# Loading the first query columns early, and scheduling with more slack behind VectorE and GpSimd, in an attention-and-mixer kernel

## The chip, the cores and the metric

The kernel runs on one core of one Trainium2 chip. The time is the device time of one execution in microseconds; the span of a profile (first to last instruction) is about 1.8 us shorter. The engines are called by the profile's names: PE (TensorE's matmuls), PEld (its weight loads), DVE (VectorE), ACT (ScalarE), POOL (GpSimd) and SP (the queue that issues most DMAs). "L829" is line 829 of the kernel.

## The reference

Sequence 2048, width 512, 32 heads of 16, everything in bf16. Two branches share x and are mixed by a gate:

```python
def reference(A_x, A_wqkv, A_wo, B_x, B_w1, B_w2, B_w3, B_w4, gate_w):
    x = A_x
    g = _sigmoid((x * gate_w).sum(-1, keepdims=True))
    a = _A_ref(x, A_wqkv, A_wo)             # 32-head attention, softmax over 2048 keys
    b = _B_ref(x, B_w1, B_w2, B_w3, B_w4)   # layernorm, w1, gelu, shift, w2, layernorm, w3, gelu, w4
    return g * a + (1 - g) * b
```

The attention's 32 x 2048 x 2048 exponentials set the size of the problem. Everything else is fitted between them.

## The kernel before

The kernel contains its own model of the engines. While it is being built, this model plays all work out in time, with a hold (how long an engine is busy) and a latency (from then until users may start) for each job, and a set of settings for each of 65 stages of the score tiles. Instructions are emitted in the order of the model's start times. Each engine's list then stands in that order; the model's times are gone, only the order stays.

```python
    def try_engine(self, e):
        # ... picks the job with the best (prio, ready, seq) among those whose inputs and buffers are there
        self.emit(self.t, j.fn)
        self.t_free[e] = self.t + j.hold
        # ...
        self.push(self.t + j.hold + j.lat, lambda: self.finish_job(j))     # users may start from here

    def dve(hold, deps, fn, **kw):
        return sim.add(Job("DVE", hold, 150.0, deps, fn, **kw))

    def act(hold, deps, fn, **kw):
        return sim.add(Job("ACT", hold, 160.0, deps, fn, **kw))

    def gp(hold, deps, fn, **kw):
        return sim.add(Job("POOL", hold, 110.0, deps, fn, port=True, **kw))
```

The scores (L829) go to two kinds of PSUM buffers. Those in "psA" get their exponential on ACT (L909). Those in "ring" are evicted by DVE (L935) as the bits of an exponential, which DVE (L971) or POOL (L974) then finishes by shifts. Both results, PA and PD, feed the value products (L1005). The first loads, and the matmuls that only keep PE busy while they run:

```python
    xa, xb = (start(e, 3000.0, lambda q, a=a: q.dma_start(out=x_sb[:, a:a + 2, :], in_=x_src(0, a, a + 2)))
              for e, a in (("SP", 0), ("ACT", 2)))
    dl_w["k0"] = start("ACT", 2300.0, col(W("k"), D, D + 128))
    dl_w["q0"] = start("ACT", 2300.0, col(wq, 0, 128))
    j_x1 = [start("SP", 4900.0, lambda q: q.dma_start(out=x_sb[:, 4:8, :], in_=x_src(1, 0, 4)))]
    # ...
    def warm_pe():
        for _ in range(8):
            nc.tensor.matmul(sim_ring[RING - 1][:, 0:384], lhsT=zero[:, 0:P], rhs=zero[:], start=True, stop=True)
```

The softmax here doesn't subtract the row's maximum and nothing guards it: scores larger than these inputs give would overflow.

Of the kernel before, what the change touches and what calls it, by code (L numbers as in the profile page):

```python
# [10 lines left out]
ACT = mybir.ActivationFunctionType  # L11
# [223 lines left out]
def kernel(  # L235
# [18 lines left out]
    S, D = x_flat.shape  # L254
# [7 lines left out]
    COL = True  # L262
# [23 lines left out]
        P1_PRIO=0.414,  # L286
        S_PRIO=0.38,
        GP2=0.0,
        GP3=1.0,
        DVE_STOP=6,  # L290
        DVE_STOP_L=8,
        URG=5,
        URG_L=17,
        DVE_ALONE=2,
        EARLY=68,
        SL=(45, 60),
        IDLE_NS=537,
        PD_LOW=0,
        PA_LOW=0,
        DVE_WAIT=3,  # L300
        AHEAD=9,
        AHEAD2=9,
        PV_FULL=0.916,
        PV_IDLE=0.37,
        PRESS=27,
        MAXU=9,
        ROT=0, DUE_SH=0, AT_SH=0,
    )
    SEG = 32
    STAGES = {0: {'DUE_SH': -20, 'AHEAD': 7, 'GP2': 0.35}, 2: {'S_PRIO': 0.324}, 3: {'SL': (125, 60), 'AT_SH': 120}, 4: {'ROT': 2, 'DVE_STOP': 7, 'DUE_SH': -8, 'GP2': 0.35}, 5: {'ROT': 2}, 6: {'AHEAD': 8, 'GP2': 0.1, 'P1_PRIO': 0.54}, 7: {'DVE_STOP': 9, 'P1_PRIO': 0.53}, 8: {'DUE_SH': 40, 'URG_L': 19, 'AT_SH': 60}, 9: {'GP2': 0.35, 'DVE_WAIT': 2, 'EARLY': 20, 'PV_IDLE': 0.245}, 10: {'GP3': 0.6}, 11: {'IDLE_NS': 706, 'GP2': 0.35}, 13: {'PV_IDLE': 0.414, 'SL': (5, 60), 'IDLE_NS': 296}, 14: {'GP3': 0.9, 'AT_SH': 120}, 15: {'ROT': 3, 'P1_PRIO': 0.554, 'PV_FULL': 0.948}, 16: {'GP2': 0.1, 'EARLY': 141}, 17: {'AT_SH': 10}, 18: {'GP2': 0.35, 'MAXU': 4}, 19: {'GP2': 0.35, 'P1_PRIO': 0.522, 'SL': (165, 180), 'DVE_WAIT': 2}, 20: {'EARLY': 145, 'S_PRIO': 0.286, 'GP2': 0.1}, 21: {'EARLY': 145, 'S_PRIO': 0.286, 'GP2': 0.1}, 22: {'AHEAD': 11, 'AT_SH': 10, 'EARLY': 51}, 23: {'AT_SH': 10}, 24: {'ROT': 2, 'URG': 3, 'GP3': 0.8}, 25: {'PD_LOW': 2}, 26: {'SL': (125, 60), 'DUE_SH': 40, 'S_PRIO': 0.248, 'AHEAD2': 8}, 27: {'ROT': 1, 'URG_L': 15, 'AHEAD': 12}, 28: {'PRESS': 21, 'P1_PRIO': 0.544, 'S_PRIO': 0.282}, 29: {'PV_IDLE': 0.462, 'DVE_STOP': 4}, 30: {'GP3': 0.9, 'PRESS': 21}, 31: {'GP3': 0.6}, 32: {'DVE_WAIT': 6, 'ROT': 2, 'DUE_SH': 40}, 34: {'DUE_SH': 40, 'DVE_ALONE': 2, 'GP3': 0.6}, 35: {'IDLE_NS': 471, 'DUE_SH': 20, 'DVE_STOP': 5, 'MAXU': 3}, 36: {'GP2': 0.1, 'PRESS': 14}, 37: {'DVE_ALONE': 2, 'DVE_STOP': 3, 'EARLY': 31, 'PA_LOW': 3}, 38: {'PD_LOW': 3, 'EARLY': 55, 'PA_LOW': 2, 'URG': 7}, 39: {'S_PRIO': 0.456, 'AHEAD2': 7, 'EARLY': 155, 'ROT': 1}, 40: {'PA_LOW': 3, 'DVE_ALONE': 2, 'GP3': 0.8}, 41: {'URG': 8, 'URG_L': 19}, 42: {'URG_L': 19, 'PRESS': 39, 'ROT': 1}, 43: {'GP3': 0.8}, 44: {'PD_LOW': 1}, 45: {'DVE_WAIT': 2, 'AHEAD2': 10}, 46: {'GP3': 0.6}, 47: {'DUE_SH': -40, 'EARLY': 79, 'MAXU': 9, 'PA_LOW': 2}, 48: {'DVE_ALONE': 300, 'ROT': 1}, 49: {'AT_SH': 120, 'P1_PRIO': 0.475}, 50: {'IDLE_NS': 896, 'PD_LOW': 2, 'ROT': 2, 'PA_LOW': 1}, 51: {'PD_LOW': 1, 'URG': 6, 'DVE_ALONE': 150, 'IDLE_NS': 830}, 52: {'PRESS': 53, 'EARLY': 6, 'IDLE_NS': 668, 'PV_FULL': 0.848}, 53: {'AHEAD': 12, 'AT_SH': 10, 'PA_LOW': 2, 'ROT': 3}, 54: {'DVE_STOP_L': 6, 'GP3': 0.9}, 55: {'DUE_SH': -40, 'PV_IDLE': 0.253, 'DVE_STOP_L': 10, 'PA_LOW': 2}, 56: {'SL': (25, 60), 'PA_LOW': 2}, 57: {'ROT': 1, 'SL': (85, 60)}, 58: {'GP3': 0.8, 'PD_LOW': 3, 'URG_L': 19}, 59: {'GP2': 0.1}, 60: {'DUE_SH': -20, 'GP3': 0.6, 'P1_PRIO': 0.409}, 61: {'GP2': 0.2}, 62: {'DVE_STOP_L': 10, 'MAXU': 6, 'PA_LOW': 2, 'AHEAD2': 11}, 63: {'DVE_STOP_L': 6, 'MAXU': 6, 'ROT': 1}, 64: {'DVE_STOP_L': 6, 'MAXU': 6, 'SL': (165, 180)}}  # L310
    K = SimpleNamespace(**BASE)


# [11 lines left out]
    def slots(name, n, shape, dt=BF16, where=const):  # L325
        return [where.tile(shape, dt, name=f"{name}{i}") for i in range(n)]
# [3 lines left out]
    wq = const.tile([P, KT, D], BF16, name="wq")  # L330
# [34 lines left out]
    sim = Sim({  # L365
        **{f"psA{w}{n}": slots(f"psA{n}", 1, [P, 512 * w], F32, ps) for n, w in enumerate(WIDTHS)},
        "ring": sim_ring,
        "PA": slots("PA", NPA, [P, 512 * max(WIDTHS)]),
        "token": list(range((NPD - 1) // 3)),
        "PD": slots("PD", NPD, [P, 1024], U16),  # L370
        "w": slots("w", NW, [P, KT, D]),
        "xnT": slots("xnT", 2, [P, KT, 512]),
        "xn": slots("xn", 2, [P, D]),
# [12 lines left out]
    })  # L386

    def dve(hold, deps, fn, **kw):
        return sim.add(Job("DVE", hold, 150.0, deps, fn, **kw))

    def act(hold, deps, fn, **kw):
        return sim.add(Job("ACT", hold, 160.0, deps, fn, **kw))

    def gp(hold, deps, fn, **kw):
        return sim.add(Job("POOL", hold, 110.0, deps, fn, port=True, **kw))

    def dma(lat, deps, fn, hold=450.0, **kw):
        return sim.add(Job("SP", hold, lat - hold, deps, fn, **kw))
# [12 lines left out]
    def W(name):  # L411
        return wb[name].slot

    j_xT, j_x, dl_w = {}, [], {}
# [9 lines left out]
    def start(eng, lat, fn, hold=530.0):  # L424

        job = sim.add(Job("SP", 1, 0.0, [], None, prio=-1))
        sim.jobs["SP"].remove(job)
        t = issue.get(eng, 700.0)
        issue[eng] = t + hold
        sim.push(t + hold + lat, lambda: sim.finish_job(job))  # L430
        sim.pending -= 1
        fn(nc.sync if eng == "SP" else nc.scalar)
        return job

    col = lambda w, n0, n1: (lambda q: q.dma_start(out=w[:, :, n0 % D:n1 if n1 <= D else (n1 - 1) % D + 1],
                                                   in_=wrows(A_wqkv[:, n0:n1])))
    xa, xb = (start(e, 3000.0, lambda q, a=a: q.dma_start(out=x_sb[:, a:a + 2, :], in_=x_src(0, a, a + 2)))
              for e, a in (("SP", 0), ("ACT", 2)))
    j_x0 = [xa, xb]
    dl_w["k0"] = start("ACT", 2300.0, col(W("k"), D, D + 128))  # L440
    dl_w["q0"] = start("ACT", 2300.0, col(wq, 0, 128))
    j_x1 = [start("SP", 4900.0, lambda q: q.dma_start(out=x_sb[:, 4:8, :], in_=x_src(1, 0, 4)))]
    dl_w["v0"] = start("SP", 2500.0, col(W("v"), 2 * D, 2 * D + 256))

# [33 lines left out]
    def ident():  # L478
        nc.gpsimd.memset(idb[:], 0.0)
        nc.gpsimd.affine_select(out=idb[:], in_=idb[:], compare_op=ALU.not_equal, fill=1.0, base=0, pattern=[[-1, P]],  # L480
                                channel_multiplier=1)

    j_id = gp(700, [], ident, prio=0)
    gp(150, [], lambda: nc.gpsimd.memset(mhalf[:], -0.5), prio=0)
    j_io = gp(200, [], lambda: nc.gpsimd.iota(mi[:], pattern=[[0, 1]], base=0, channel_multiplier=1), prio=0)
    j_z = dve(300, [], lambda: nc.vector.memset(zero[:], 0.0), prio=0)
    j_idf = gp(300, [j_id], lambda: nc.gpsimd.tensor_copy(out=idf[:], in_=idb[:]), prio=7)
    j_wl = gp(500, [], lambda: nc.gpsimd.memset(woL[:], 0.0), prio=7)
# [4 lines left out]
    act(1450, [j_z], lambda: nc.scalar.activation(out=zc[:, 0:1], in_=zero[:, 0:1], func=ACT.Exp), prio=0)  # L493

    def warm_pe():
        for _ in range(8):
            nc.tensor.matmul(sim_ring[RING - 1][:, 0:384], lhsT=zero[:, 0:P], rhs=zero[:], start=True, stop=True)

    sim.emit(350.0, warm_pe)
    j_m1 = dve(100, [j_io], lambda: nc.vector.tensor_scalar(out=mb[:], in0=mi[:], scalar1=16, scalar2=None,  # L500
                                                            op0=ALU.bitwise_and), prio=0)
# [24 lines left out]
        return g  # L526

    def evac(g, hold, fn, prio=2, eng="DVE", **kw):
        job = Job(eng, hold, 150.0, [g.units[-1][-1]] if not COL else g.units[-1], lambda: fn(g.buf.slot), prio=prio,
                  frees=[g.buf] + kw.pop("frees", []), **kw)  # L530
        return sim.add(job)

# [21 lines left out]
    def k_proj(G, c, at):  # L554
        g = gen(f"k{G}", at, [j_xT[c, 0, k] for k in range(KT)] + [dl_w["k0" if G == 0 else "k"]],
                [(lambda a, b, k=k: W("k")[:, k, G * P + a:G * P + b],
                  lambda k=k: W(f"x{c}0")[:, k, :]) for k in range(KT)])
        g.ops[-1].frees += [wb["k"], wb[f"x{c}0"]]
        if G == 0 and c == 0:
            g.due = -3  # L560
            j_k[G, c] = act(500, g.units[-1], lambda: nc.scalar.copy(out=kT[G][:, 0:512], in_=g.buf.slot[:]), prio=0,
                            frees=[g.buf])
            return
        g.due = 14 * c - 6 if G == 0 else g.due
        j_k[G, c] = evac(g, PSUM_NS, lambda ps: nc.vector.tensor_copy(out=kT[G][:, c * 512:(c + 1) * 512], in_=ps[:]),
                         prio=1)
# [595 lines left out]
    def pe_pick():  # L1162
        t = sim.t
        if sim.tiles // SEG != stage[0]:
            stage[0] = sim.tiles // SEG
            K.__dict__.update({**BASE, **STAGES.get(stage[0], {})})

# [153 lines left out]
    for tt in range(4):  # L1321
        t = NT - 4 + tt
        o = (sim.free["ot"] + sim.free["xn"])[tt]
        for j in range(4):
            nc.tensor.matmul(bank[tt][32 * j:32 * j + 32, :], lhsT=oT[:, tt * P + 32 * j:tt * P + 32 * j + 32], rhs=woL[:],
                             start=False, stop=True, tile_position=(0, 32 * j), skip_group_check=True)
# [35 lines left out]
```

## Time and profile before

| | before |
|---|---|
| time, median of 3 | 788.51 us (787.51 to 789.9) |
| span of the profile | 787.5 us |
| first score matmul, first main exponential | 13.44, 14.50 us |
| from the first to the end of the last main exponential (the body) | 763.2 us |
| from there to the end (the tail) | 9.8 us |

In the page's part of costliest groups, a row has line, engine, operation, tiles and shapes, the count, then busy us and mean ns of one, then the engine's idle time just before these instructions with what ended most of it:

```profile
L909 ACT ACTIVATE PA<-psA 128x1024 bf16<-128x1024 f32 x739 | 693.4, 1040 | 25.0 <-PE acc L1005 8.7
L935 DVE TENSOR_SCALAR PD<-ring 128x512 uint16<-128x512 f32 x570 | 374.4, 682 | 17.8 <-PE ring L829 15.0
L519 PE MATMUL ring<-w,wq 128*32 128x512 bf16 x256 | 21.2, 398 | 2.8 <-DMA wq<-in_A_wqkv_dram 2.3
```

The exponentials alone fill ACT for 693 us. The eviction row shows DVE's largest idle time, behind score matmuls. The third row has the load that the change moves: PE stood 2.3 us for the first columns of wq, once. The waits: us in total, times, longest.

```profile
DVE xn L682 <- DMA xn_dram<-xn: 1.6, 1, 1.6
```

### The profile page before, as it was taken

What the parts mean: (1) busy time and instruction counts of PE and PEld (TensorE: products, weight loads), DVE (VectorE), ACT (ScalarE), POOL (GpSimd) and SP (SyncE); (2) the same over time, 40 slices, a digit from 0 to 9 for tenths busy, and PEclk for the clock granted to TensorE, in tenths of its full rate; (3) what the DMA queues carried; (4) which work ended last, traced back from release to release, by engine and by line L of the source; (5) the groups of instructions that cost most, each with busy time, mean ns of one, the idle gap of its engine ahead of it and who ended that gap; (6) DMA issues with size and microseconds to landing.
All of it is one profiled execution on the core that took longest, in us unless ns stands there. A gap on an engine that the chain in (4) does not pass through costs nothing.

```text
span 787.5 us, 23893 instructions
## 1 busy us (share of the span) xinstructions
PE 766.7 (97%) x9672; PEld 227.1 (29%) x9672; DVE 744.9 (95%) x1587; ACT 743.3 (94%) x764; POOL 339.2 (43%) x331
## 2 busy tenths in 40 slices
PE   7999999999999999999999999999999999999997
PEld 3433322222222222223222223222223222223222
DVE  4999999999999999999998999899999999999996
ACT  4899999999999999999999999999999999999995
POOL 2234544344546443444244443344434345445352
PEclk9999999999999999999999999999999999999999
DMA  8302113423000320062101001001100000000101
GB/s 204 123 16 46 37 46 80 91 45 113 20 6 20 83 59 20 25 152 62 29 11 32 23 20 46 19 18 36 43 18 20 15 22 26 26 20 20 17 6 44
DMA packets 67093, 34.60 MB, mean 44 GB/s; under 512 B 46748, under 2 KB 62380, under 8 KB 66984
## 3 DMA queue, kind: packets, MB, share of 16 engines
q1 hardware_dynamic: 65512, 32.43, 16.7%
q8 instruction: 75, 1.23, 0.7%
q10 hardware_dynamic: 1472, 0.66, 0.3%
q14 instruction: 34, 0.28, 0.1%
HBM read 17.40 MB, written 6.81 MB: 31 GB/s over the span
## 4 chain that ended last, share of the span: by engine, by line
PE 57%; DVE 23%; ACT 12%; issue 3%; DMA 3%; SPq 1%; POOL 0%; ACTq 0%; POOLq 0%; DVEq 0%
PE acc L1005 20%; PE ring L519 18%; PE psA L829 18%; DVE PD L935 9%; ACT PA L909 9%; DVE PD L971 7%; DMA xn_dram<-xn 1%; PE ring L829 1%; DVE st L662 1%; DMA wq<-in_A_wqkv_dram 1%; DVE V L605 1%; ACT hT L722 1%; ACT hT L753 1%; ACT hB L753 1%; DVE hB L752 1%
## 5 line engine op out<-in xcount | busy, mean ns | idle before, releaser
L909 ACT ACTIVATE PA<-psA 128x1024 bf16<-128x1024 f32 x739 | 693.4, 1040 | 25.0 <-PE acc L1005 8.7
L974 POOL TENSOR_SCALAR PD<-PD 128x1024 uint16<-128x1024 uint16 x269 | 283.8, 1058 | 418.2 <-DVE PD L971 263.0
L935 DVE TENSOR_SCALAR PD<-ring 128x512 uint16<-128x512 f32 x570 | 374.4, 682 | 17.8 <-PE ring L829 15.0
L1005 PE MATMUL acc<-PD,V 128*17 128x512 bf16 x2280 | 302.3, 381 | 2.6 <-DVE accsb L1021 1.4
L829 PE MATMUL psA<-q,kT 32*128 32x512 bf16 x1478 | 284.7, 384 | 3.4 <-ACT PA L909 3.1
L1005 PE MATMUL acc<-PA,V 128*17 128x512 bf16 x1478 | 269.7, 381 | 0.2 <-DVE accsb L1021 0.2
L971 DVE TENSOR_SCALAR PD<-PD 128x1024 uint16<-128x1024 uint16 x586 | 241.4, 453 | 3.5 <-PE acc L1005 1.7
L829 PE MATMUL ring<-q,kT 32*128 32x512 bf16 x570 | 195.4, 384 | 2.8 <-DVE PD L935 2.5
L829 PEld LDWEIGHTS <-kT 32*128 32x128 bf16 x2048 | 73.9, 91 | 306.2 <-issue 305.1
L1005 PEld LDWEIGHTS <-V 128*17 128x17 bf16 x3758 | 74.4, 88 | 141.3 <-issue 119.7
L519 PE MATMUL ring<-xnT,w 128*32 128x512 bf16 x1152 | 91.4, 383 | 1.9 <-DVE qf L588 1.5
L519 PE MATMUL ring<-w,hT 128*32 128x512 bf16 x704 | 58.2, 383 | 0.2 <-DVE PD L935 0.2
L519 PEld LDWEIGHTS <-w 128*32 128x32 bf16 x1920 | 43.5, 95 | 49.7 <-issue 37.8
L1038 POOL TENSOR_TENSOR oT<-accsb,bcs 128x512 bf16<-128x512 f32 x31 | 40.3, 1301 | 10.9 <-DMA bcs<-rr 7.5
L519 PE MATMUL ring<-w,w 128*32 128x256 bf16 (+1 forms) x768 | 41.0, 316 | 0.8 <-DVE PD L935 0.8
L519 PE MATMUL ring<-w,hB 128*32 128x512 bf16 x448 | 35.1, 383 | 0.0
L519 PE MATMUL ring<-w,wq 128*32 128x512 bf16 x256 | 21.2, 398 | 2.8 <-DMA wq<-in_A_wqkv_dram 2.3
L1021 DVE COPY accsb<-acc 128x512 f32<-128x512 f32 x31 | 21.1, 682 | 1.5 <-POOL oT L1038 0.9
L662 DVE BATCH_NORM_STATS2 st<-x_sb 128x6 f32<-128x512 bf16 x32 | 21.6, 682 | 0.0
L519 PEld LDWEIGHTS <-hT 128*32 128x32 bf16 x704 | 14.7, 95 | 19.3 <-issue 14.7
L752 DVE CAST hB<-ring 128x512 bf16<-128x512 f32 x28 | 18.9, 680 | 0.8 <-PE ring L519 0.7
L752 DVE CAST hT<-ring 128x512 bf16<-128x512 f32 x28 | 19.0, 684 | 0.2 <-PE ring L519 0.2
(93 smaller groups left out, 285.2 us busy)
## 6 DMA issues: line engine op xcount, KB each, us to landing
bcs<-rr SPq DMA_DIRECT2D x124, 64.0 KB
xn_dram<-xn SPq DMA_DIRECT2D x32, 128.0 KB
w<-in_B_w_dram SPq DMA_DIRECT2D x5, 512.0 KB
oD<-oT SPq DMA_DIRECT2D x124, 16.0 KB
w<-in_B_w_dram SPq DMA_DIRECT2D x4, 448.0 KB
out_dram<-ot SPq DMA_DIRECT2D x14, 128.0 KB
x_sb<-in_A_x_dram SPq DMA_DIRECT2D x3, 512.0 KB
w<-in_A_wqkv_dram SPq DMA_DIRECT2D x2, 256.0 KB
```

Of the source, the lines that this page charges most:

```text
L519: units.append([Op("col", j, lambda j=j, lf=lf, rf=rf, n0=n0, n1=n1, st=st, sp=sp: nc.tensor.matmul(get()[32 * j:32 * j + 32, n0:n1], lhsT ...
L662: a = dve(600, deps, lambda: nc.vector.bn_stats(out=sb.slot[:], in_=x_sb[:, t, :]), prio=6, at=at, acq=[sb])
L752: pre.append(evac(g, PSUM_NS, lambda ps, m=m: nc.vector.tensor_copy(out=h2()[:, m, :], in_=ps[:])))
L753: ge = act(93 + 427 * FT + 2600, pre, lambda: nc.scalar.activation(out=h2(), in_=h2(), func=ACT.Gelu_apprx_tanh), prio=0)
L829: o = Op("row", i, lambda: nc.tensor.matmul(dst(), lhsT=kT[G][32 * i:32 * i + 32, kt * P:(kt + 1) * P], rhs=qbuf[G, c].slot[32 * i:32 * i ...
L909: job = act(hold, ops, lambda: nc.scalar.activation(out=pb.slot[:, 0:n], in_=buf.slot[:, 0:n], func=ACT.Exp, scale=0.25), acq=[pb], frees= ...
L935: nc.vector.tensor_scalar(out=pr["buf"].slot[:, h * 512:(h + 1) * 512], in0=buf.slot[:], scalar1=BITS_MUL, scalar2=BITS_ADD, op0=ALU.mult, ...
L971: nc.vector.tensor_scalar(out=d[k][:, 0:w], in0=d[0][:, 0:w], scalar1=float(SHIFT * k), scalar2=None, op0=ALU.add)
L974: nc.gpsimd.tensor_scalar(out=d[k][:, 0:w], in0=d[0 if both else 2][:, 0:w], scalar1=1.0, scalar2=float(SHIFT * (k if both else 1)), op0=A ...
L1005: o = Op("col", i, lambda: nc.tensor.matmul(acc[32 * i:32 * i + DH + 1, :], lhsT=lhs(), rhs=rhs(), start=st, stop=True, tile_position=(0, ...
L1021: e = dve(PSUM_NS, round_ops[r], lambda: nc.vector.tensor_copy(out=ab.slot[:], in_=acc[:]), acq=[ab], prio=0)
L1038: n = gp(1250, d3, lambda: nc.gpsimd.tensor_tensor(out=ob.slot[:], in0=ab.slot[:], in1=bb.slot[:], op=ALU.mult), acq=[ob], frees=[ab, bb], ...
```

## The change

Its intent has two parts. The first 128 columns of the query weights, which the first scores need, go out second on SP's queue instead of third on ACT's, with three more warm-up matmuls. And the model holds results of DVE and POOL back longer before their users may start (280 and 250 ns for 150 and 110), so that on the chip the users should find them ready; with that, the settings of the stages were chosen anew, so the order of the whole program is new.

```diff
-    STAGES = {0: {'DUE_SH': -20, 'AHEAD': 7, 'GP2': 0.35}, 2: {'S_PRIO': 0.324}, ... }      # cut: 65 stages
+    STAGES = {0: {'AHEAD': 6, 'EARLY': 13, 'DVE_ALONE': 150, 'S_PRIO': 0.368}, ... }        # cut
     def dve(hold, deps, fn, **kw):
-        return sim.add(Job("DVE", hold, 150.0, deps, fn, **kw))
+        return sim.add(Job("DVE", hold, 280.0, deps, fn, **kw))
     def gp(hold, deps, fn, **kw):
-        return sim.add(Job("POOL", hold, 110.0, deps, fn, port=True, **kw))
+        return sim.add(Job("POOL", hold, 250.0, deps, fn, port=True, **kw))
-    dl_w["k0"] = start("ACT", 2300.0, col(W("k"), D, D + 128))
-    dl_w["q0"] = start("ACT", 2300.0, col(wq, 0, 128))
+    dl_w["q0"] = start("SP", 2600.0, col(wq, 0, 128))
+    dl_w["k0"] = start("ACT", 2900.0, col(W("k"), D, D + 128))
     def warm_pe():
-        for _ in range(8):
+        for _ in range(11):
     def evac(g, hold, fn, prio=2, eng="DVE", **kw):
-        job = Job(eng, hold, 150.0, ...)      # cut
+        job = Job(eng, hold, 280.0, ...)      # cut
```

## The prediction

> **What bounds the kernel now.** First the page, part 1, the busy shares of the engines:
>
> ```profile
> PE 766.7 (97%) x9672; PEld 227.1 (29%) x9672; DVE 744.9 (95%) x1587; ACT 743.3 (94%) x764; POOL 339.2 (43%) x331
> ```
>
> Three engines are above 94%, so no single busy share names the bound, and GpSimd (POOL) is not it. Next, the busy sums by stretch, cut at the first and at the end of the last of the main exponentials (14.5 and 777.7 us); after the first number the columns are PE, PEld, DVE, ACT, POOL busy with counts, then clock, DMA share, GB/s:
>
> ```profile
> 0.00:14.50 14.50, 10.30 (x77) 4.98 (x77) 3.65 (x10) 4.10 (x7) 3.87 (x14) 1.00 0.98 226
> 14.50:777.70 763.20, 750.79 (x9524) 219.08 (x9525) 737.20 (x1570) 737.95 (x756) 335.31 (x317) 1.00 0.16 40
> 777.70:787.50 9.80, 5.62 (x81) 3.00 (x70) 4.02 (x8) 1.29 (x3) 0.00 (x0) 1.00 0.16 54
> ```
>
> The span is a head of 14.5 us, a body of 763.2 and a tail of 9.8. In the body ACT idles 763.2 - 738.0 = 25.2 us and DVE 26.0. That is all the slack there is: even with no idle on ACT the span would be 14.5 + 738.0 + 9.8 = 762 us, 3.2% less.
>
> PE's busy time is no measure, since the ends of its matmuls are modelled. I took the starts of the single matmuls from the trace. Within the body a change from scores (line 829, row tiles) to column work (lines 519, 1005) takes 0.315 us from start to start, back again 0.312 us, and a further group of four column tiles 0.2155 us: a change of mode costs about 0.097 us beside 0.2155 us of streaming. Laying the program's own order of matmuls with these three numbers and no waits gives 730.1 us from the first score to the last value product; the trace has 765.4 us. So PE too is full to 95%, with some 35 us of gaps. For each late start I compared the ends of the instructions whose semaphores it waits for: 79 late starts (22.0 us together) stand 0.051 to 0.053 us after the end of a DVE instruction, 11 (3.0 us) as close after a GpSimd one, 41 (7.7 us) after an ACT one; the rest has no such neighbour. The timeline shows one:
>
> ```profile
> 772.64 1.87 DVE L935 TENSOR_SCALAR PD<-ring 128x512 uint16<-128x512 f32 x3
> ...
> 773.37 0.37 PE L829 MATMUL ring<-q,kT 32*128 32x512 bf16 x1 [0.27 <-DVE PD L935]
> 773.67 0.11 PEld L1005 LDWEIGHTS <-V 128*17 128x17 bf16 x8 [0.87 <-issue]
> ```
>
> The first of the three DVE evictions ends near 773.32 (one lasts 0.68); 0.05 us later PE may write the ring bank again, and the eight value products behind it stood in line. Last, who ACT and DVE waited for:
>
> ```profile
> ACT PA L909 <- PE acc L1005: 8.7, 25, 1.1
> ACT PA L909 <- PE ring L829: 7.2, 14, 1.2
> ACT PA L909 <- PE psA L829: 6.6, 12, 1.5
> DVE PD L935 <- PE ring L829: 15.0, 36, 1.8
> ```
>
> They wait for PE, which waits for them: the bound is one coupled loop of three nearly full engines, each in program order, and each late hand-over stops everything behind it.
>
> The head, by the timeline:
>
> ```profile
> 1.12 2.74 PE L497 MATMUL ring<-zero 128*128 128x384 bf16 x8 [1.12 <-DVE zero L486]
> 1.80 0.56 ACTq L435 DMA_DIRECT2D wq<-in_A_wqkv_dram  x1
> 4.61 2.00 PE L539 MATMUL ring<-idb,x_sb 128*128 128x128 bf16 x16 [0.75 <-DMA x_sb<-in_A_x_dram]
> 6.65 0.76 DVE L548 COPY w<-ring 128x512 bf16<-128x512 bf16 x2 [4.50 <-PE ring L539]
> 8.94 1.90 PE L519 MATMUL ring<-w,wq 128*32 128x512 bf16 x16 [2.33 <-DMA wq<-in_A_wqkv_dram]
> 10.62 1.92 PE L519 MATMUL ring<-w,w 128*32 128x512 bf16 x16
> 14.50 6.54 ACT L909 ACTIVATE PA<-psA 128x1024 bf16<-128x1024 f32 x7
> ```
>
> The transposed x is ready at 7.41, the first q columns at 8.9. And the 32 projection matmuls take 3.60 us, 0.45 us per group of four, twice the 0.2155 of the body: the trace's clock records grant full speed only from 13.37 us.
>
> **What the Trainium skill says.** (1) "Perfetto Trace Analysis", section Per-instruction lifecycle: a DVE or ACT record ends when the write is acknowledged, and the semaphore's way to the other engines comes after it, unseen. The trace agrees and sizes it: 0.05 us. (2) "TensorE: Matmul & The Clock Gate", Part 2: weight loads may be pulled ahead, but matmuls stay in program order. The trace agrees (the line at 773.67 stands behind 773.37). (3) Same page, Part 1: PE starts at half clock and is let go after about one busy window of 3.4 us. The trace agrees in kind: half rate until 13.37, 4.4 us after work without a pause begins at 8.94. (4) "DMA: Bandwidth & Descriptors", Queues, rings and completion order: each DMA engine takes turns between the queues, in order within one. The trace's packets agree: ACT's queue moved the 256 B packets of k and then q between 4.3 and 8.0 us while SP's moved others.
>
> **The change part by part.** (a) *Head.* The order of instructions shows the q columns now second on SP's queue, ahead of the 512 KB of x, no longer third on ACT's. Both queues then have 512 packets of 256 B behind x, which is through at about 4.3 us. In the trace ACT's queue took some 370 such packets per us beside SP's, so about 1.4 us: through at 5.7. The old q was through at 8.0 and used at 8.94; with the same 0.9 us it is usable at 6.6, before 7.41. So q can start at 7.46: 1.48 us earlier. (b) Three more warm-up matmuls (11, not 8) of 0.34 us: PE is busy to 1.12 + 11 x 0.34 = 4.9, 0.3 us beyond where the transposes now start (4.61), so q starts near 7.6-7.75. In return PE is busy without a pause from 1.1 to 6.9 us, longer than the 4.4 us that sufficed later, so I give 70% that q and k run at full clock: 8 groups x (0.45 - 0.2155) = 1.9 us less. Head: 1.3 us cold, 3.2 warm; 0.7 x 3.2 + 0.3 x 1.3 = 2.6, and I take 2.3, since loads behind q come 0.5 us later on SP's queue.
>
> (c) *Slack.* The scheduler's model now holds the result of a DVE instruction back 280 ns after its hold instead of 150, of a GpSimd one 250 instead of 110. No instruction gets slower; PE is merely given other work first. If each of the 79 late starts behind DVE lost up to 0.13 us, that is 8.9 us (many are shorter), and of the 11 behind GpSimd 1.3: 10.2 us at most. ACT's 160 is untouched, and so are its 7.7 us. (d) *Work,* counted from the order of both programs: ACT gets 741 exponentials of 1024 columns and one of 512 for 739: about 2.5 x 0.938 us = +2.4 us (693.4/739 each). DVE loses 5 evictions at 0.657 (374.4/570) and net 10 - 3/2 shifts at 0.412 (241.4/586): -6.8 us. GpSimd +1 of 269. PE: 15 value products and 72 fillers fewer, but 1490 runs of one mode for 1483; laid as above without waits, 731.2 us for 730.1: +1.1 us. So ACT becomes the fullest, 740.4 us, with room for at most 23 us of gain in the body.
>
> **Sum.** I count half of the 10.2, because a wait taken from PE partly comes back as a wait for ACT, which gets fuller: -5.1. PE work +1.1, head -2.3: -6.3. 788.5 - 6.3 = 782.2 us.
>
> **Rivals.** *The slack costs what it saves.* Results used 130 ns later hold ring banks and PD buffers longer, and all stage settings were chosen anew; DVE idling 15.0 us on ring scores speaks for it. Body unchanged, the head alone: 786. *ACT as the bound.* It gains 2.4 us of work and its own hand-overs get no slack; with its 25 us idle kept, body 765.6 and total 788.5 + 2.4 - 2.3 = 788.6. Against it: its idle time is behind PE, which is what improves. *The full gain:* all 10.2 and a warm head of 3.2: 788.5 - 10.2 + 1.1 - 3.2 = 776. *The head hidden anyway:* later loads (the rest of k, v) could set the first 30 us; DMA is 0.98 busy up to 14.5 us, which speaks for it; then 784.5. Against it, no wait for them stands among the longest.
>
> **Range and chances.** The full gain gives the low end, 776; no gain in the body plus a small head, 787.5. Faster by over 2% means below 772.7: the full gain and 3 us beyond; 4%. Slower by over 2% needs 804; 1%. Within 2%: 95%.
>
> **What would show it.** q's first matmul near 7.6 instead of 8.94 and the first exponential at 11.3 (warm) or 13.2 (cold). Fewer late PE starts behind DVE: some 79 to about 40, 22 us to about 13; those behind ACT unchanged or more. ACT's idle time in the body from 25 to about 19 us. Matmul gaps of 0.315 and 0.312 us unchanged. Wrong if the body keeps its 763 us, or if the new order lets PE wait less than half as much (below 776).

## More of the kernel before

The layer norm writes its result into one of two "xn" buffers, from which a DMA stores it; only when the store has landed is the buffer free:

```python
            xb = Buf("xn", 1)                                   # one of two
            g = dve(323, [m], lambda t=t, xb=xb: nc.vector.tensor_scalar(
                out=xb.slot[:], in0=x_sb[:, t, :], ...), prio=0.35, acq=[xb], port=True)       # L682
            ds.append(dma(2200.0, [g], lambda t=t, xb=xb: nc.sync.dma_start(
                out=xn_dram[which, t * P:(t + 1) * P, :], in_=xb.slot[:]), frees=[xb]))
```

## The result, and the profile after

The changed kernel takes 782.58 us (median of 4, 782.21 to 783.01), the kernel before 788.26 us beside it: ratio 0.9925, 95% interval 0.9908 to 0.9942. A second set of five, measured later, gave 0.9936 (0.9923 to 0.9948). A ratio is the mean time of one kernel's runs over that of the other's of the same rounds, so it is not quite the ratio of the medians quoted.

The page after, its first part and the groups that answer to those of before:

```profile
PE 765.1 (98%) x9588; PEld 227.1 (29%) x9588; DVE 740.0 (95%) x1575; ACT 744.4 (95%) x767; POOL 341.5 (44%) x332
...
L909 ACT ACTIVATE PA<-psA 128x1024 bf16<-128x1024 f32 x742 | 694.5, 1040 | 23.1 <-PE psA L829 8.5
...
L935 DVE TENSOR_SCALAR PD<-ring 128x512 uint16<-128x512 f32 x565 | 372.6, 680 | 23.4 <-PE ring L829 21.6
...
L519 PE MATMUL ring<-w,wq 128*32 128x512 bf16 x256 | 20.9, 383 | 0.7 <-DVE PD L935 0.4
```

The wait for wq is gone. ACT's idle time has hardly moved (25.0 to 23.1 us), and DVE's before its evictions has grown (17.8 to 23.4). The busy sums by stretch, cut at the same two events as in the prediction (columns: stretch, PE, PEld, DVE, ACT, POOL busy with counts, clock, DMA share, GB/s):

```profile
0.00:9.71 9.71, 8.23 (x78) 4.68 (x79) 3.45 (x10) 4.07 (x8) 3.88 (x14) 1.00 0.95 213
9.71:772.10 762.39, 752.05 (x9449) 220.59 (x9447) 732.52 (x1558) 739.08 (x759) 337.63 (x318) 1.00 0.16 42
772.10:781.10 9.00, 4.84 (x67) 1.87 (x64) 4.02 (x8) 1.27 (x2) 0.00 (x0) 0.94 0.18 60
```

So the 6.4 us of span are 4.8 in the head (14.50 to 9.71), 0.8 in the body (763.20 to 762.39) and 0.8 in the tail (9.80 to 9.00). The head, by the timeline (start, us, engine, line, operation, tiles; in brackets the idle time before it and what ended that):

```profile
1.12 3.70 PE L497 MATMUL ring<-zero 128*128 128x384 bf16 x11 [1.12 <-DVE zero L486]
...
1.26 0.45 SPq L435 DMA_DIRECT2D wq<-in_A_wqkv_dram  x1
...
4.61 1.33 PE L539 MATMUL ring<-idb,x_sb 128*128 128x128 bf16 x16
...
5.54 1.07 ACT L548 COPY w<-ring 128x512 bf16<-128x512 bf16 x2 [2.24 <-PE ring L539]
...
6.18 1.12 PE L519 MATMUL ring<-w,wq 128*32 128x512 bf16 x16 [0.23 <-ACT w L548]
...
9.71 5.62 ACT L909 ACTIVATE PA<-psA 128x1024 bf16<-128x1024 f32 x6
```

The q matmuls now start 0.23 us after the transposes and wait for the first copy of x (ACT w), not for a load. They take 1.12 us instead of 1.90; the trace's clock records have full speed from 5.18 us instead of 13.37. The waits after:

```profile
ACT PA L909 <- PE psA L829: 8.5, 12, 2.4
ACT PA L909 <- PE acc L1005: 7.8, 15, 2.1
...
ACT PA L909 <- PE ring L829: 4.1, 10, 0.7
```

```profile
DVE PD L935 <- PE ring L829: 21.6, 57, 1.1
```

The three waits of ACT sum to 20.4 us against 22.5 before. DVE waits for ring scores 57 times instead of 36. The late starts of PE, taken from the trace as in the prediction (over 20 ns late, and within 0.06 us after the end of the instruction waited for):

| late starts behind | before | after |
|---|---|---|
| DVE | 79, 21.4 us | 78, 19.2 us |
| POOL | 11, 3.0 us | 1, 0.6 us |
| ACT | 40, 7.6 us | 55, 8.7 us |
| no such neighbour | 81, 11.3 us | 90, 13.6 us |

(The prediction's sums for before, 22.0 and 7.7 us, and its 41, are of a slightly different cut; both columns here use the same one.) POOL's late starts have gone; DVE's have not. The sums of a column come to more than the prediction's 35 us of gaps, which is not explained here, so go by the direction: counted by a simpler rule (first matmul of each group, from the first score to the last value product) they are 60 before and 52 after behind DVE, 9 and 1 behind POOL.

### The profile page after: what moved, and what is told of

The parts are those of the page before. It is cut to its first block, busy times and chain, and to the rows that moved or that the text cites. A ratio compares the mean times of both kernels' runs of the same rounds, so it can differ in the third digit from the quotient of the medians.

```text
span 781.1 us, 23746 instructions
## 1 busy us (share of the span) xinstructions
PE 765.1 (98%) x9588; PEld 227.1 (29%) x9588; DVE 740.0 (95%) x1575; ACT 744.4 (95%) x767; POOL 341.5 (44%) x332
## 4 chain that ended last, share of the span: by engine, by line
PE 54%; DVE 29%; ACT 10%; issue 4%; DMA 1%; SPq 0%; DVEq 0%; ACTq 0%
PE acc L1005 19%; PE psA L829 17%; PE ring L519 16%; DVE PD L935 12%; DVE PD L971 10%; ACT PA L909 6%; ACT hB L753 2%; ACT hT L753 2%; DVE x_sb L731 1%; DVE st L662 1%; PE ring L829 1%; DVE xn L682 1%; DVE hB L752 1%; DVE accsb L1021 1%; ACT L909 1%
## 5 line engine op out<-in xcount | busy, mean ns | idle before, releaser
L909 ACT ACTIVATE PA<-psA 128x1024 bf16<-128x1024 f32 x742 | 694.5, 1040 | 23.1 <-PE psA L829 8.5
L935 DVE TENSOR_SCALAR PD<-ring 128x512 uint16<-128x512 f32 x565 | 372.6, 680 | 23.4 <-PE ring L829 21.6
L1005 PE MATMUL acc<-PD,V 128*17 128x512 bf16 x2260 | 308.9, 381 | 3.8 <-DVE PD L971 2.2
L1005 PE MATMUL acc<-PA,V 128*17 128x512 bf16 x1483 | 278.6, 381 | 0.0
L829 PE MATMUL ring<-q,kT 32*128 32x512 bf16 x565 | 191.6, 384 | 0.9 <-DVE PD L935 0.9
L519 PE MATMUL ring<-xnT,w 128*32 128x512 bf16 x1152 | 88.5, 383 | 0.2 <-DVE PD L935 0.2
L1038 POOL TENSOR_TENSOR oT<-accsb,bcs 128x512 bf16<-128x512 f32 x31 | 42.0, 1356 | 9.8 <-DMA bcs<-rr 9.8
```

The lines of the kernel that those rows point to most:

```text
L519: units.append([Op("col", j, lambda j=j, lf=lf, rf=rf, n0=n0, n1=n1, st=st, sp=sp: nc.tensor.matmul(get()[32 * j:32 * j + 32, n0:n1], lhsT ...
L829: o = Op("row", i, lambda: nc.tensor.matmul(dst(), lhsT=kT[G][32 * i:32 * i + 32, kt * P:(kt + 1) * P], rhs=qbuf[G, c].slot[32 * i:32 * i ...
L909: job = act(hold, ops, lambda: nc.scalar.activation(out=pb.slot[:, 0:n], in_=buf.slot[:, 0:n], func=ACT.Exp, scale=0.25), acq=[pb], frees= ...
L935: nc.vector.tensor_scalar(out=pr["buf"].slot[:, h * 512:(h + 1) * 512], in0=buf.slot[:], scalar1=BITS_MUL, scalar2=BITS_ADD, op0=ALU.mult, ...
L1005: o = Op("col", i, lambda: nc.tensor.matmul(acc[32 * i:32 * i + DH + 1, :], lhsT=lhs(), rhs=rhs(), start=st, stop=True, tile_position=(0, ...
L1038: n = gp(1250, d3, lambda: nc.gpsimd.tensor_tensor(out=ob.slot[:], in0=ab.slot[:], in1=bb.slot[:], op=ALU.mult), acq=[ob], frees=[ab, bb], ...
```

## The experiments

**Head and order, apart.** Two kinds of kernel could be made without touching the rest. In the kernel before, the load's place in the queue and the warm-ups can be changed while the model keeps its old times, so that the order of everything else stays word for word:

```diff
-    dl_w["q0"] = start("ACT", 2300.0, col(wq, 0, 128))
+    dl_w["q0"] = start("ACT", 2300.0, lambda q: col(wq, 0, 128)(nc.sync))      # h_move, h_both
-        for _ in range(8):
+        for _ in range(11):                                                   # h_warm, h_both
```

And in the changed kernel the old head can be put back under the new order (a_oldhead):

```diff
-    dl_w["q0"] = start("SP", 2600.0, col(wq, 0, 128))
     dl_w["k0"] = start("ACT", 2900.0, col(W("k"), D, D + 128))
+    dl_w["q0"] = start("SP", 2600.0, lambda q: col(wq, 0, 128)(nc.scalar))
-        for _ in range(11):
+        for _ in range(8):
```

h_both, the whole new head under the old order:

> The order of the kernel before on every engine, word for word, with only the change's two head edits: the load of the q columns is second on SP's queue instead of third on ACT's, and there are 11 warm-up matmuls instead of 8. Theory 1 (the gain of the change is its head; its new order for the body gives nearly nothing): first exponential near 9.7 us instead of 14.5, and 783.0 to 784.2 us against 788.3, a gain of 4.1 to 5.3 us. Rival (a lead in the head is given back within the first 50 us, because the later loads of k, v and x set the pace, and the change's gain is its new order in the body): first exponential early too, but the time stays at 786.5 to 788.5 us.

h_move, the load alone:

> As the run with both head edits, but the moved load alone, 8 warm-up matmuls. Theory 1a (the load and the clock each give about half): q starts near 6.5 us, transposes and the first part of q run at half clock, first exponential at 11.5 to 12.5 us, time 785.3 to 786.5. Rival 1b (the moved load is all of it, the warm-up nothing): first exponential at 9.7 to 10.2, time as with both edits, 783.0 to 784.2.

h_warm, the warm-ups alone:

> As the run with both head edits, but the 3 further warm-up matmuls alone; the load of q stays third on ACT's queue. q still starts at 8.9 us. Theory 1a: the clock is granted in full near 5.2 us and holds over the pause until 8.9, so q and k take 1.7 us instead of 3.6, first exponential near 12.6, time 786.2 to 787.0. Rival 1c (the pause of some 2.9 us drops the clock again, or the warm-up does nothing by itself): first exponential at 14.5, time 788.0 to 788.8.

a_oldhead, the new order alone:

> The order of the changed kernel on every engine, word for word, with the old head: q third on ACT's queue and 8 warm-up matmuls. Theory 1 (the head is the gain): 786.7 to 788.0 us, that is 0.3 to 1.6 us under the kernel before and 4 to 5 us over the changed one. Rival (the new order of the body is the gain): 783 to 784.5 us, less than 2 us over the changed kernel. The prediction on record (head 2.3, body 4.0) expects 784.9.

Measured together on one chip, five rounds; the kernel before took 788.63 us there:

| | time, us | ratio | 95% interval |
|---|---|---|---|
| h_both | 786.34 | 0.9974 | 0.996 to 0.9987 |
| h_move | 784.44 | 0.9959 | 0.9939 to 0.998 |
| h_warm | 789.78 | 1.0013 | 0.9994 to 1.0031 |
| a_oldhead | 788.01 | 0.9994 | 0.998 to 1.0007 |

Under the old head the new order is worth nothing that can be measured. The load alone does at least what the whole head does (the intervals of h_move and h_both overlap), the warm-ups alone nothing. Against what was expected: h_both fell between its theory (783.0 to 784.2) and its rival (786.5 to 788.5), close to the rival; h_move came close to rival 1b, a_oldhead to theory 1; h_warm has about the time of rival 1c, but its trace is nearer to theory 1a, as shown below. The timeline of h_move has the early start with 8 warm-ups:

```profile
4.17 1.69 PE L539 MATMUL ring<-idb,x_sb 128*128 128x128 bf16 x16 [0.32 <-DMA x_sb<-in_A_x_dram]
...
6.09 1.13 PE L519 MATMUL ring<-w,wq 128*32 128x512 bf16 x16 [0.22 <-ACT w L548]
...
9.63 6.54 ACT L909 ACTIVATE PA<-psA 128x1024 bf16<-128x1024 f32 x7
```

and a_oldhead, where the load comes late:

```profile
4.29 1.28 PE L539 MATMUL ring<-idb,x_sb 128*128 128x128 bf16 x16 [0.43 <-POOL woL L488]
...
8.20 1.90 PE L519 MATMUL ring<-w,wq 128*32 128x512 bf16 x16 [2.63 <-DMA wq<-in_A_wqkv_dram]
```

In a_oldhead PE had already reached full clock at 4.64 us (its transposes took 1.28 us), then stood 2.63 us for wq; the clock records go back to half at 8.05 and to full at 11.47, steps of 3.41 us, and the q matmuls run at half rate. The Trainium skill, "TensorE: Matmul & The Clock Gate", Part 1, gives the window over which the clock is decided as 3413 ns and free-running; the trace agrees with these steps. The early load removes the pause, and with it, here, the second fall of the clock. The records of six kernels have full speed from 4.64, 5.18, 5.30, 6.10, 7.12 and 13.37 us: when it comes differs from execution to execution, and with the pause it can come as late as 13.

A pause does not always bring the fall. The profiled execution of h_warm, with the late load, kept full speed from 7.12 us on, through a pause of 1.98 us:

```profile
8.51 1.05 PE L519 MATMUL ring<-w,wq 128*32 128x512 bf16 x16 [1.98 <-DMA wq<-in_A_wqkv_dram]
...
11.97 4.71 ACT L909 ACTIVATE PA<-psA 128x1024 bf16<-128x1024 f32 x5
```

The mean clocks say what is usual. With the early load (h_both, h_move, and below h_both_again and a_w8, and the changed kernel in both sets: 32 executions) the mean is 0.999 or 1.000 in every one. With the late load (the kernel before in the three sets of experiments, h_warm, a_oldhead: 41) it is 0.998 or less in 28, in h_warm in four of six. One fall for 3.41 us takes about 0.002 off the mean, by an estimate from the span. (h_both_xn3, below, is left out: its clock falls late in the program.) Where the clock fell in executions that were not profiled is not on record.

With 11 warm-ups the two single effects do not add up. Head alone under the old order is 0.9974, order alone 0.9994: together 0.9968, or 786.1 us of 788.6. Both together were 0.9925 and 0.9936. About 3 us of this head's gain appear only under the new order. With 8 warm-ups they do add up: the load alone is 0.9959, times 0.9994 makes 0.9953, and a_w8 below, the load under the new order, measured 0.9948. So the early load does not need the new order; whether the eleven warm-ups really harm the old order and help the new is within the noise of single pairs of runs.

**Where the old order loses the head's lead.** I lined up the starts of the same score tiles (0 to 2047) in each trace. This is how many us each is ahead of the kernel before:

| score tile | 0 | 400 | 800 | 1400 | 1800 | 2047 |
|---|---|---|---|---|---|---|
| h_both | 4.2 | 4.3 | 3.0 | 2.5 | 2.6 | 2.6 |
| h_warm | 2.3 | 3.1 | 1.7 | 0.5 | 0.5 | 0.5 |
| h_move | 4.7 | 6.1 | 5.1 | 5.2 | 5.3 | 5.1 |
| a_oldhead | 1.0 | 1.7 | -2.2 | 1.5 | 0.3 | 0.4 |
| changed kernel | 4.6 | 6.7 | 2.7 | 6.3 | 5.1 | 5.4 |

The first three have the same order as the kernel before, so a change of lead is a wait gained or lost. In h_both and h_warm DVE stands 4.2 and 3.7 us for the stores that free the layer norm's two buffers, in h_move 1.7, before 1.6; under the new order it never does. That suggested a test: the old order with the new head, run again for a pair (h_both_again), and the same with three buffers in rotation (h_both_xn3). There is no room for a third buffer, so I used the tile of the last weights, and its clearing and four small loads were put near the end of the program instead of its start:

```diff
+    xn3 = sim.free["xn"][:2] + [woL]             # taken in turn by the layer norm and its store
-                out=xb.slot[:], in0=x_sb[:, t, :], ...
+                out=xbuf(xb, t)[:], in0=x_sb[:, t, :], ...
-    j_wl = gp(500, [], lambda: nc.gpsimd.memset(woL[:], 0.0), prio=7)      # and its 4 loads
+    j_wl = gp(500, [], lambda: None, prio=7)
+    sim.emit(tl - 80000.0, late_wo)              # the clearing and the 4 loads, 80 us before the model's end
```

h_both_again:

> The order of before with the whole new head once more, so that the next run has its pair on the same chip. Expected as measured: ratio 0.9974, about 786.0 us, with VectorE waiting some 4 us for the stores that free the two buffers of the layer norm.

h_both_xn3:

> The same order again, but the layer norm's result goes round three buffers in place of two (the third is the last weights' tile, which is filled late for it); nothing else moves on any engine but those loads. Theory (in the old order the head's lead is lost because VectorE comes to the layer norm sooner and then waits for a store to free a buffer): the 4 us of such waits go to under 0.5, the lead over the kernel before stays near 4 us instead of 2.5, and the time falls by 1 to 2.5 us, to 783.5 to 785. Rival (the lead is lost to hand-overs that land differently, the waits for stores being by the way): unchanged within 0.5 us of its pair.

Measured on one chip, five rounds: h_both_again 786.05 us, ratio 0.9973 (0.996 to 0.9986); h_both_xn3 786.62 us, 0.9979 (0.9965 to 0.9993). By the total, the theory failed: no gain. The traces say more. In h_both_again DVE stands three times for a store:

```profile
140.66 0.74 DVE L682 TENSOR_SCALAR xn<-x_sb,rs,nm 128x512 bf16<-128x512 bf16 x2 [1.60 <-DMA xn_dram<-xn]
...
262.58 0.69 DVE L682 TENSOR_SCALAR xn<-x_sb,rs,nm 128x512 bf16<-128x512 bf16 x1 [0.68 <-DMA xn_dram<-xn]
...
330.01 0.41 DVE L682 TENSOR_SCALAR xn<-x_sb,rs,nm 128x512 bf16<-128x512 bf16 x1 [1.63 <-DMA xn_dram<-xn]
```

In h_both_xn3 no layer norm waits for a store. Its lead is 4.0, 6.2, 4.6, 6.0, 6.1 us at the tiles 0, 400, 800, 1400, 1800, where its pair has 4.8, 5.4, 4.2, 2.6, 2.7. So far as the theory says. But within 8 us, between 697 and 705, it loses 2.45 us again and ends with 3.7. That is just behind the place where my edit put the loads (its lines are numbered up to 9 higher; L838 is the score matmul, L944 the eviction, L980 the shift):

```profile
690.95 0.52 POOL L1311 MEMSET woL<- 128x512 bf16 x1
...
691.50 1.71 SPq L1313 DMA_DIRECT2D woL<-in_A_wo_dram  x4
...
693.25 0.42 SPq L1044 DMA_DIRECT2D bcs<-rr  x1
...
695.24 3.35 DVE L980 TENSOR_SCALAR PD<-PD 128x1024 uint16<-128x1024 uint16 x4
695.34 1.44 POOL L1047 TENSOR_TENSOR oT<-accsb,bcs 128x512 bf16<-128x512 f32 x1 [1.26 <-DMA bcs<-rr]
...
699.23 0.37 PE L838 MATMUL ring<-q,kT 32*128 32x512 bf16 x1 [1.22 <-DVE PD L944]
...
701.49 1.02 ACT L918 ACTIVATE PA<-psA 128x1024 bf16<-128x1024 f32 x1 [2.08 <-PE ring L838]
```

Read downwards: SP's queue issues my four loads before the last of four bcs loads, so this one comes late, POOL waits 1.26 us for it (in the pair it does not wait), and its multiplication now runs into DVE's shifts. Four shifts take 3.35 us (2.27 in the pair); one of them, from 695.57, takes 1.50 us where most take 0.42, and ends 0.29 us after POOL's instruction. The Trainium skill, "SBUF — State Buffer", section "SBUF: two separate sides", says that GpSimd and DVE, in some of its modes, share a port pair as an exclusive lock that is held for the whole instruction; this agrees in kind. The next eviction is late, PE waits 1.22 us, ACT 2.08. And then a second cost (columns as above; the last but two is the clock):

```profile
692.80:696.20 3.40, 3.40 (x46) 0.84 (x38) 3.40 (x7) 3.39 (x5) 1.90 (x2) 1.00 0.11 34
696.20:699.60 3.40, 2.18 (x28) 0.57 (x28) 3.40 (x5) 3.21 (x4) 2.50 (x3) 1.00 0.07 18
699.66:703.07 3.41, 3.41 (x23) 0.59 (x17) 3.18 (x7) 1.04 (x2) 1.19 (x2) 0.50 0.03 7
703.10:706.50 3.40, 3.40 (x42) 0.83 (x38) 2.90 (x7) 3.34 (x4) 1.04 (x1) 1.00 0.01 2
```

After a stretch in which PE was busy for 2.18 of 3.40 us, the clock is at half for 3.41 us, and PE does 23 matmuls there instead of some 45. The mean clock of h_both_xn3's six executions is 0.996 to 0.998 in five, 0.999 to 1.000 in all five of its pair; its one execution at 1.000 was its fastest, 784.67 us. So the trace supports the theory up to 690 us, and the run as a whole does not prove it, because my own edit, in the one execution that was traced, cost about what the theory promised. One execution at 784.67 is no proof either.

**Eleven warm-ups or eight.** a_w8 is the changed kernel with 8, and the changed kernel was run again beside it (after_again).

```diff
-        for _ in range(11):
+        for _ in range(8):
```

> The changed kernel once more, for an interval on the same chip as the other three. Every theory expects the ratio to the kernel before that it had: 0.9925, so 782 to 783 us.

> The changed kernel with 8 warm-up matmuls in place of 11 (q still second on SP's queue). The warm-ups beyond 8 gave nothing with the old order (moved load alone 784.4, with 11 warm-ups 786.3). Theory A (with q early PE is busy without a pause anyway, and three more warm-ups only delay the transposes): 0 to 0.8 us faster than the changed kernel, 781.5 to 783, with the first exponential at 9.4 to 9.8 us. Theory B (the eleven are what gives full clock early): full clock only from about 7 to 8.5 us, the first exponential at 10.5 to 12 us, and 1 to 2 us slower, 783.5 to 785.

Measured, same chip and rounds as the pair above: after_again 782.74 us, 0.9936 (0.9923 to 0.9948); a_w8 783.89 us, 0.9948 (0.9934 to 0.9963). The intervals overlap. In a_w8's profile the transposes start at 4.08 and the first exponential at 9.84, about as theory A has it (9.4 to 9.8), but the time is not better, against theory A, and lies in the range of theory B (783.5 to 785). Its profiled execution was one of its slower ones (785.1 us; the six go from 782.4 to 785.9). That the eleven help is possible and not shown. No kernel I ran beats the changed one.

**The slack, apart from the settings.** The stage settings were searched for one pair of latencies, so neither can be changed alone without spoiling the other. I ran both mixtures and two kernels without any stage settings; all four have the new head:

```diff
 # a_lat_old: the changed kernel with the old latencies (150/110), new STAGES
-        return sim.add(Job("DVE", hold, 280.0, deps, fn, **kw))      # and evac
+        return sim.add(Job("DVE", hold, 150.0, deps, fn, **kw))
-        return sim.add(Job("POOL", hold, 250.0, deps, fn, port=True, **kw))
+        return sim.add(Job("POOL", hold, 110.0, deps, fn, port=True, **kw))
 # a_stages_b: the changed kernel (280/250) with the STAGES of before
 # u_150, u_280: the changed kernel with STAGES = {} and the latencies 150/110 and 280/250
```

> The changed kernel with the slack taken back: the model holds DVE's results back 150 ns and GpSimd's 110 instead of 280 and 250; new head and new stage settings stay. The settings were found for the larger slack, so the order gets worse whatever the slack is worth: its matmuls laid without waits take 744.8 us in the body, 13.6 more than those of the changed kernel. Theory M (slack and settings only work as a matched pair): 792 to 800 us. Rival S (the settings hardly matter, the slack hardly either): within 3 us of 782.6.

> The changed kernel with the stage settings of the kernel before: new head, new slack, old settings. Laid without waits the body's matmuls take 750.0 us. Theory M: 795 to 805 us, so worse than the kernel before in spite of the head. Rival S: the slack with any settings is good for 4 us, 782 to 786 us.

> New head, no stage settings at all (the base values throughout), old slack of 150 and 110 ns. With the next run it compares the slack alone, neither being tuned. Laid without waits the body's matmuls take 748.5 us. Theory N (slack by itself neither saves nor costs over 3 us in the body, since what PE no longer waits for DVE comes back as other waits): within 3 us of the next run beyond what the laid-out work differs (748.5 against 744.6). More than 90 late PE starts behind DVE and GpSimd in the profile, against some 60 in the next. Both 795 to 805 us.

> New head, no stage settings, new slack of 280 and 250 ns. Theory S1 (slack takes PE's waits away, as the prediction had it): late PE starts behind DVE and GpSimd fewer than two thirds of those of the run with 150 and 110 ns, and time lower by 5 us or more, of which 3.9 are laid-out work. Theory N: late starts as many or nearly so, time within 3 us of it beyond the laid-out work.

Measured on one chip, three rounds, the kernel before at 787.94 us: a_lat_old 808.91 (1.0264), a_stages_b 820.3 (1.0411), u_150 817.7 (1.0375), u_280 823.62 (1.0451). All intervals are within 0.004 of these. All four were slower than every theory had expected (805 us at most). Settings and latencies that do not match, or no settings, cost 26 to 41 us against the changed kernel, several times the whole change. With no settings, more slack is slower by 6 us, so both theories for that pair failed: N expected u_280 to be 3.9 us faster, give or take 3, and S1 at least 5 us faster. These runs cannot give the slack's own worth; what they give is a look at the model. I recorded the model's own times for each of these programs while it was built, and set them beside the traces, from the first score to the start of the last value product:

| order | latencies | model, us | chip, us | chip over model, us |
|---|---|---|---|---|
| before (and h_both, h_move, h_warm, h_both_again: 15.6 to 18.4) | 150/110 | 749.2 | 765.2 | 16.0 |
| a_lat_old | 150/110 | 772.5 | 790.4 | 17.9 |
| u_150 | 150/110 | 784.9 | 798.3 | 13.3 |
| changed (and after_again, a_w8, a_oldhead: 7.1 to 10.4) | 280/250 | 754.9 | 763.3 | 8.4 |
| u_280 | 280/250 | 797.2 | 803.0 | 5.8 |
| a_stages_b | 280/250 | 782.0 | 799.8 | 17.8 |

The model's own plan got 5.7 us longer (749.2 to 754.9) and came true 7.6 us better (16.0 to 8.4): net about 2. In two of three sets of settings slack goes with a truer plan (the new ones, 17.9 to 8.4, and none, 13.3 to 5.8). The third, the settings of before (16.0, and 17.8 in a_stages_b), contradicts it: there PE stood once for 4.0 us behind an eviction, the clock fell for 3.41 us, and the chip was 17.8 us over the plan in spite of the slack. So "slack makes the plan truer and longer, and the two nearly cancel" fits the change's own pair; as a rule it is not shown.

## Why the prediction was right, and where its steps were wrong

The total was right: 782.2 predicted, 782.58 and 782.74 measured. By the traces its two large terms were both wrong, in opposite directions, so that it came so close is luck. By the times alone the split depends on which part is put in first: head first, 2.1 us (h_both, 0.9974) and 3 to 4 for the order, which is the prediction's own split; order first, 0.5 us (a_oldhead, 0.9994) and 4.6 to 5.4 for the head. What speaks against the prediction's split is the mechanism of each term:

- **Head, -2.3: mis-sized.** The first exponential came at 9.71, not at 11.3 (warm) or 13.2 (cold): 4.8 us, and 5.4 at the last score tile. The failing step was "q can start at 7.46": I took q to need all four transposed slices of x (ready at 7.41), but its first matmuls need only the first copied slice, and in the new trace they start at 6.18, 0.64 us after that copy began. The load itself was mis-sized too, at "some 370" packets per us and through at 5.7: in the trace before, the 1024 packets of 256 B on ACT's queue take from 4.45 to 8.23 us, about 270 per us, and in the new one q's 512 packets go through on SP's queue from 3.75 to 4.47 us. The other step was the clock. I gave full speed to the q and k matmuls only (1.9 us, times 0.7); the transposes had it in part (records from 5.18 us; 1.33 us for 2.00). And I counted on the three more warm-ups for it. The runs point to the load instead: h_move has it with 8 warm-ups, and with 11 and the late load four of six executions of h_warm lost clock.
- **Slack, -5.1: mis-sized.** "If each of the 79 late starts behind DVE lost up to 0.13 us", half of it counted. They are 78 after, 19.2 us for 21.4. For POOL the step held: 11 to 1. The forecast of "about 40" was wrong, and ACT's idle time fell to 23.1, not 19. In all, under the old head the new order measured 0.9994, 0.5 us with an interval of about 1.1 either way, where the prediction's terms for it (-5.1 and +1.1) make 4.0. A late start is not a property of the hand-over alone. Which engine is late is decided in a loop in which each waits for the others, and DVE now waits for PE 57 times instead of 36. That this loop used up the slack is my reading of these two numbers, not something that a run isolates.
- **Work.** The +1.1 us of PE is a sum that no run tests by itself; the gaps of 0.315 and 0.312 us on which it rests are the same after. The counts were right (742 exponentials, 565 evictions, 579 shifts by DVE), their times less so: ACT's busy time grew by 1.1 us, not 2.4, and DVE's fell by 4.9, not 6.8.
- **The rivals.** "Slack costs what it saves" had the body right (763.2 to 762.4) and was wrong at 786 only because it used the same small head. "ACT as the bound" did not happen: ACT's idle time fell a little while its work grew. "The head hidden anyway" is half true, and of the old order: there the head's lead of 4 to 5 us ends as 2.4 to 5.1, with waits for the layer norm's buffers in the traces where it shrinks. In both traces of the changed kernel all of it reaches the end; in a_w8's, 4.5 us end as 3.3.
- **Tail, 0.8 us:** not predicted, and not tested.

## What to carry to other kernels

A pause in front of the first real matmuls can cost twice: the wait itself, and the clock that falls during it; here the early load was worth more than more warm-up work. In a loop of nearly full engines, a count of late hand-overs is not a sum of savings: test what an order change alone is worth, by putting the other parts back. When an experiment moves something out of the way, look at the trace where it was put: here, in the one trace, four small loads on a busy queue cost as much as the effect under test.

## What the Trainium skill lacked or had wrong

- "TensorE: Matmul & The Clock Gate", section "Why this matters for your kernels", says that idle gaps over about 3 us between bursts of matmuls drop the clock, after a window of idle. (Elsewhere the page says that frequent short idle times can do it too, without a length.) Here far shorter gaps did: in h_both_xn3 a start of PE that was 1.22 us late, in a stretch with PE busy 2.18 of 3.40 us, was followed by 3.41 us at half clock. In a_lat_old it happened twice, at 346 and 442 us, after windows with PE busy for 71% and 62%. A window with 55% in the kernel before, ending at 488 us, was not followed by a fall, so busy time as recorded is not the whole rule.
- "Perfetto Trace Analysis", section "Per-instruction lifecycle", places the semaphore's way after the recorded end of an instruction, but gives no figure: from the end of a DVE, ACT or POOL record to the start of the PE instruction that waited, the traces have 0.050 to 0.053 us.
- "TensorEngine Tiling (Array Packing)", section "Key Properties", says that a change of tiling mode drains TensorE, without a figure. Here a change between row tiles and column tiles costs about 0.1 us, beside 0.2155 us for a group of four tiles of 512 columns (0.312 to 0.315 us from start to start, before and after the change).
- No page says that a profile's mean clock leaves out the time before the first record: the page before shows full clock in every slice, while its records begin only at 13.37 us and its matmuls ran at half rate until then.
